# Six attention units ahead of the first half steps, a bank reserve in the planner, decays by doubling and spare buffers at the end, in a decay-attention kernel with a softplus feed-forward layer

## The chip, the core and the metric

The kernel runs on one core of a Trainium2 chip. The core has five engines with queues of their own: TensorE (PE; its weight loads are listed apart as PEld), VectorE (DVE), ScalarE (ACT), GpSimd (POOL), and SyncE (SP), which here only issues DMAs. They wait for each other by semaphores. The metric is the device time of one execution in microseconds. Before the change it was 692.98 us, the median of three runs (692.51 to 694.04).

## The reference

```python
def _attn_ref(q, k, v):                      # B, H, S, D = 4, 8, 768, 64
    gamma = 1.0 - 2.0 ** (-5.0 - np.arange(H, dtype=np.float32))
    scale = 1.0 / np.sqrt(D)
    for t in range(S):
        state = gamma[None, :, None, None] * state + np.einsum('bhd,bhe->bhde', k[:, :, t], v[:, :, t])
        y[:, :, t] = scale * np.einsum('bhd,bhde->bhe', q[:, :, t], state)

def _moe_ref(x, w_in, w_out):                # x: 3072 x 512, w_in: 512 x 2048, w_out: 2048 x 512
    h = x @ w_in
    g = np.maximum(h, 0.0) + np.log1p(np.exp(-np.abs(h)))
    return g @ w_out
```

The attention's output, heads side by side, is `x`. The weights come as 64-bit floats and are turned into float32 words on the chip.

## The kernel before

**Attention in units.** The 768 positions are cut into six chunks of 128 (`C`), the eight heads into two halves of four. A unit is one chunk of one batch for one half: 4 x 6 x 2 = 48 units, `u0` to `u47`, two of them (the two halves) per chunk. In a unit GpSimd scales the queries and values by powers of the decay (L348, from `qtabs` and `vtabs`, one column per chunk), TensorE transposes keys and queries (L356), the scores of the chunk are formed, copied out, masked by GpSimd (L388, L448), and multiplied with the values; the product with the state of the chunks before (`st`) is added. The state is carried on in `td` (L481 to L502). The outputs go to `x` as a high and a low part (L473 ScalarE, L474 VectorE), since the feed-forward layer multiplies in three products: high by high, low by high, high by low, all in float32r.

The first `WHOLE` = 14 units multiply in float32; the others split their operands into two float32r parts as well (the `else` branch of `unit`: L412 to L421 and L444 to L448), with more matmuls, each a quicker one, and more work for ScalarE, VectorE and GpSimd.

**Feed-forward in steps.** The 3072 rows are six blocks of 512 (`T`), the 2048 hidden columns sixteen pieces `f` of 128. A step is one block and one `f`: 12 matmuls of 512 columns into one of two banks `hp0`, `hp1`; then VectorE (L539), ScalarE's softplus (L540), VectorE (L541), ScalarE's cast to `gh` (L542) and GpSimd's rest `gl` (L543); then 12 matmuls with `w_out` into the banks `acc0` to `acc3`. There is one `sp` buffer between L539 and L543 and two each of `gh` and `gl`. After a block's last step the banks are copied to `w0` or `w1` (L576 ScalarE, L578 VectorE) and stored (L580).

In block 0 the first steps are half steps: two `f` at once for the first (`h0`) or second (`h1`) half of the rows, with matmuls of 256 columns, so that they can begin when four of the block's eight units are there. The weights of an `f` are converted just ahead of its first use (L287 to L318: loads, ScalarE, VectorE, GpSimd).

**The order is planned.** Nothing is emitted directly. Every operation is given to a `Planner` with its engine, a cost, the operations it comes after, the buffers it uses (`Held`) and, for some, a due time. `order()` then works out due times backwards, and places one operation after the other by a model of costs and hand-over times (`HANDOVER`, the functions for the costs, the DMA rate): the engine that can begin first, and on it the operation that is due first. That sequence is emitted, and each engine's queue keeps it. Some banks (`SHARED`) are taken by whichever operation comes first. So a change of a cost or a due time moves instructions on every engine, and a line of code may be used at another place than its neighbours.

The list `ORDER` (L24) gives the due times of block 0's first units and half steps one after the other; behind it the main loop gives one step at a time, with new units as the blocks need them.

Of the kernel before, what the change touches and what calls it, by code (L numbers as in the profile page):

```python
# [17 lines left out]
P = 128  # L18
# [3 lines left out]
WHOLE = 14  # L22
BORROW = 8
ORDER = ("u0", "u1", "u2", "u3", "u4", "h0", "u5", "h0", "u6", "u7", "h1", "h1")  # L24
# [8 lines left out]
    "SP": {"PE": 150, "ACT": 30, "DVE": 30, "POOL": 140, "SP": 0},  # L33
# [46 lines left out]
class Planner:  # L80
# [5 lines left out]
    def add(self, engine, cost, run, after=(), uses=(), at=None):  # L86
        op = Op(engine, cost, run, after, uses, at)
        op.number = len(self.ops)
        self.ops.append(op)
        return op  # L90

    def order(self):
# [28 lines left out]
        while len(out) < len(self.ops):  # L121
            best = None
            for e, cands in ready.items():
                if not cands:
                    continue
                starts = []
                for since, op in cands:
                    b = begin(op, since)
                    starts.append((max(free[e], b), b, op))
                first = min(c[0] for c in starts)  # L130
                if first >= 1e12 or best is not None and first >= best[0]:
                    continue
                s, b, op = min((c for c in starts if c[0] <= first + 1e-6), key=lambda c: (c[1] + COMFORT[e] > c[0], c[2].due, c[2].number))
                best = s, op
# [9 lines left out]
            if e == "SP":  # L144
                free[e] = s + 450
                lane = max(lane, s + 2000 - 0.3 * op.cost) + op.cost + (190 if op.cost < 500 else 0)
                op.end = lane + 150
            else:
                op.end = free[e] = s + op.cost
# [5 lines left out]
            for t in op.then:  # L155
                waiting[t] -= 1
                if not waiting[t]:
                    ready[t.engine].append((max(a.end + HANDOVER[a.engine][t.engine] + (MARGIN if a.engine != t.engine else 0) for a in t.after), t))
# [4 lines left out]
SLOW = 1.02  # L163
SHARED = ("hp0", "hp1", "acc0", "acc1", "acc2", "acc3", "a0", "a1")
COMFORT = {"PE": 0, "ACT": 100, "DVE": 100, "POOL": 100, "SP": 0}
# [3 lines left out]
def decay_attention_then_softplus_ffn(ctx: ExitStack, tc: tile.TileContext, q, k, v, w_in, w_out, qtab, vtab, gtab, out):  # L169
# [42 lines left out]
    gtab_sb = pool.tile([P, 2, H], F32, name="gtab_sb")  # L212
    qtabs = pool.tile([P, NC, H], F32, name="qtabs")
    vtabs = pool.tile([P, NC, H], F32, name="vtabs")
# [52 lines left out]
    def DMA(size, run, after=(), uses=(), at=None):  # L267
        return plan.add("SP", size / 316.0, run, after, uses, at)
# [57 lines left out]
    zero, ys, ss, padded = [], {}, {}, []  # L326

    def unit(n, when):
# [16 lines left out]
        ldq = DMA(4 * P * HH * D, lambda: emit(nc.sync.dma_start(buf(qn), src(q))), [], [qn], when[0] - 6000)  # L345
        ldk = DMA(4 * P * HH * D, lambda: emit(nc.sync.dma_start(buf(kn), src(k))), [], [kn], when[0] - 6000)
        ldv = DMA(4 * P * HH * D, lambda: emit(nc.sync.dma_start(buf(vn), src(v))), [], [vn], when[0] - 6000)
        scaled = lambda t, tab: emit(nc.gpsimd.tensor_tensor(t, t, tab[:, c, hs].unsqueeze(2).broadcast_to([P, HH, D]), op=ALU.mult))  # L348
        dq = POOL(615, lambda: scaled(buf(qn), qtabs), [ldq] + tables, [qn])
        dv = POOL(615, lambda: scaled(buf(vn), vtabs), [ldv] + tables, [vn])  # L350
# [56 lines left out]
        else:  # L407
# [3 lines left out]
            for par, own, oth in sides:  # L411
                ck.append(ACT(scalar_time(512), lambda par=par, own=own: emit(nc.scalar.copy(KQ[int(kq.slot[-1])][own, par, :2], tpv()[own])), [tk, tq], [tp, kq]))  # L412
# [5 lines left out]
            vl = DVE(vector_time(256), lambda: emit(nc.vector.tensor_tensor(buf(vhl)[:, :, 1, :], buf(vn), buf(vhl)[:, :, 0, :].bitcast(F32), op=ALU.subtract)), [vh], [vn, vhl])  # L418
            if not ends:
                khi = ACT(scalar_time(256, False), lambda: emit(nc.scalar.copy(buf(kh), buf(kn))), [ldk], [kn, kh])  # L420
                klo = DVE(vector_time(256), lambda: emit(nc.vector.tensor_tensor(buf(kl), buf(kn), buf(kh).bitcast(F32), op=ALU.subtract)), [khi], [kn, kh, kl])  # L421
# [72 lines left out]
        else:  # L494
# [6 lines left out]
                DVE(vector_time(128), lambda: emit(nc.vector.tensor_tensor(buf(to)[up, 0], tdv[:, 0], buf(to)[lo, 0].bitcast(F32), op=ALU.subtract)), [h0], [to]),  # L501
                DVE(vector_time(128), lambda: emit(nc.vector.tensor_tensor(buf(to)[lo, 1], tdv[:, 1], OD.bitcast(F32), op=ALU.subtract)), [h1], [to, od]),  # L502
# [8 lines left out]
    accs = {}  # L511

    def ffn_step(s, h, i, f, when):
# [5 lines left out]
        gl = hold_gl()  # L519
        ts = range(NT) if h is None else range(h * W // P, (h + 1) * W // P)  # L520
# [18 lines left out]
        a = DVE(vector_time(T), lambda: emit(nc.vector.tensor_scalar(U(spv()), U(bank(hp)), 0x80000000, None, op0=ALU.bitwise_or)), [lasts[-1]], [hp, sp])  # L539
# [43 lines left out]
    def setup_tables():  # L583
        emit(nc.scalar.dma_start(qtabs[:, 0], qtab))
        emit(nc.scalar.dma_start(vtabs[:, 0], vtab))
        emit(nc.scalar.dma_start(gtab_sb[lo, 0], gtab))
# [101 lines left out]
```

## Time and profile before

| | before |
|---|---|
| median of 3 runs | 692.98 us (692.51 to 694.04) |
| profiled execution | 691.09 us, its span 689.4 us |
| TensorE busy | 671.6 us, 97% of the span |
| VectorE, ScalarE, GpSimd busy | 413.3, 358.7, 276.8 us |
| matmul rows | 3952, of them 1104 + 96 into `hp`, 768 + 384 into `acc` from `gh` and `gl` |
| bytes moved | 42.67 MB, 62 GB/s in the mean |

The page's busy times are unions of rows. Matmuls are pipelined, so a row's own length (390 ns for 512 columns) is longer than the distance to the next (some 0.23 us); the distance between starts is what a matmul costs its engine. In a timeline a row gives start, length, engine, line, operation, what is written and read, shapes and count, and in brackets the idle time before it with what ended it. Names are the program's tiles: `a`, `acc`, `hp` are banks of the accumulator memory, `win` and `wout` the converted weights, whose last two pieces lend their buffers to early loads, so `wout<-in_q_dram` is a load of queries.

### The profile page before, as it was taken

The page shows a single profiled execution, that of the slowest core. Times are in us where ns is not written, and L with a number is a line of the kernel's source. Part 1 is how long each engine was busy: PE and PEld are TensorE (multiplying, and loading weights), DVE is VectorE, ACT ScalarE, POOL GpSimd, SP SyncE. Part 2 cuts the span into 40 slices and gives each one's busy share as a digit, 9 for nine tenths or more (in the row PEclk, how much of TensorE's full clock was granted, in tenths as well). Part 3 has the DMA queues.
Part 4 walks back from the last instruction along what each step waited for, and adds up shares of the span by engine and source line. Part 5 has one row for each costly group of instructions (what it writes and reads, how often), then busy time and mean ns, then how long its engine had stood idle before and what let it go on. Part 6 is the DMA issues. An engine that isn't in the chain of part 4 may idle for free. (4 is left out here: it accounts for less than half of the span.)

```text
span 689.4 us, 11100 instructions
## 1 busy us (share of the span) xinstructions
PE 671.6 (97%) x3952; PEld 561.8 (82%) x3952; DVE 413.3 (60%) x867; ACT 358.7 (52%) x799; POOL 276.8 (40%) x320
## 2 busy tenths in 40 slices
PE   6998999999999999999999999999999999999995
PEld 5887888888888888888888888888888888888883
DVE  4877867768665656756657656666766564322222
ACT  5887767656555445545545554554645443322222
POOL 5866756543434343433333343333433322222221
PEclk9999999999999999999999999999999999999999
DMA  9859363223111112211111311111211000100001
GB/s 240 225 155 298 92 200 107 53 47 93 24 30 40 24 23 57 75 25 24 39 30 24 93 39 24 24 34 37 85 24 41 21 1 1 52 10 1 1 1 61
DMA packets 90743, 42.67 MB, mean 62 GB/s; under 512 B 77376, under 2 KB 85568, under 8 KB 90688
## 3 DMA queue, kind: packets, MB, share of 16 engines
q1 hardware_dynamic: 90240, 41.96, 22.2%
q8 instruction: 31, 0.51, 0.3%
q14 instruction: 24, 0.20, 0.1%
q10 hardware_dynamic: 448, 0.01, 0.0%
HBM read 35.66 MB, written 6.29 MB: 61 GB/s over the span
## 5 line engine op out<-in xcount | busy, mean ns | idle before, releaser
L270 PE MATMUL hp<-x,win 128*128 128x512 f32 (+1 forms) x1200 | 297.7, 388 | 2.6 <-DVE sp L541 1.6
L270 PEld LDWEIGHTS hp<-x,win 128*128 128x128 f32 x1200 | 213.4, 188 | 42.8 <-issue 2.9
L270 PE MATMUL acc<-wout,gh 128*128 128x512 f32 x768 | 202.3, 395 | 1.4 <-ACT gh L542 1.4
L543 POOL TENSOR_TENSOR gl<-sp,gh 128x512 fp32r<-128x512 f32 x96 | 124.5, 1297 | 186.5 <-ACT gh L542 106.0
L270 PEld LDWEIGHTS acc<-wout,gh 128*128 128x128 f32 x768 | 139.4, 188 | 29.7 <-ACT gh L542 2.3
L539 DVE TENSOR_SCALAR sp<-hp 128x512 uint32<-128x512 uint32 x96 | 65.8, 686 | 92.4 <-PE hp L270 53.1
L540 ACT ACTIVATE sp<-sp 128x512 f32<-128x512 f32 x96 | 60.6, 631 | 100.9 <-DVE sp L539 100.7
L270 PE MATMUL acc<-wout,gl 128*128 128x512 f32 x384 | 108.8, 391 | 0.7 <-POOL gl L543 0.7
L270 PEld LDWEIGHTS acc<-wout,gl 128*128 128x128 f32 x384 | 71.2, 188 | 15.7 <-POOL gl L543 1.1
L542 ACT CAST gh<-sp 128x512 fp32r<-128x512 f32 x96 | 59.5, 619 | 35.8 <-DVE sp L541 35.3
L541 DVE SCALAR_TENSOR_TENSOR sp<-hp,sp 128x512 f32<-128x512 f32 x96 | 66.1, 688 | 17.6 <-ACT sp L540 16.0
L444 ACT CAST ah<-a 128x256 fp32r<-128x256 f32 x68 | 23.0, 375 | 64.8 <-PE a L270 64.4
L414 DVE TENSOR_TENSOR kq<-a,kq 64x256 fp32r<-64x256 f32 x68 | 28.7, 422 | 45.5 <-ACT kq L413 37.8
L448 POOL TENSOR_SCALAR_AFFINE_SELECT ah<-ah 128x512 fp32r<-128x512 f32 x34 | 21.9, 644 | 75.2 <-DVE al L445 75.2
L412 ACT CAST kq<-a 64x512 fp32r<-64x512 f32 x68 | 39.5, 581 | 22.9 <-PE a L356 17.2
L348 POOL TENSOR_TENSOR vn<-vn,vtabs 128x256 f32<-128x256 f32 x46 | 28.6, 621 | 49.5 <-DMA vn<-in_v_dram 30.5
L348 POOL TENSOR_TENSOR qn<-qn,qtabs 128x256 f32<-128x256 f32 x46 | 28.5, 620 | 47.3 <-DMA qn<-in_q_dram 42.6
L445 DVE TENSOR_TENSOR al<-a,ah 128x256 fp32r<-128x256 f32 x68 | 26.7, 419 | 34.6 <-ACT ah L444 34.3
L270 PE MATMUL a<-ah,vhl 128*64 128x128 f32 x272 | 40.8, 222 | 0.0
L474 DVE TENSOR_TENSOR x<-a,x 64x256 fp32r<-64x256 f32 x86 | 35.8, 416 | 8.4 <-ACT x L473 7.1
L270 PE MATMUL a<-kq,st 128*64 128x128 f32 x240 | 34.1, 223 | 0.0
L473 ACT CAST x<-a 64x256 fp32r<-64x256 f32 x86 | 31.4, 365 | 5.0 <-PE a L270 3.1
(121 smaller groups left out, 831.2 us busy)
## 6 DMA issues: line engine op xcount, KB each, us to landing
raw<-in_moe_w_in_dram SPq DMA_DIRECT2D x16, 512.0 KB, 5.3
raw<-in_moe_w_out_dram SPq DMA_DIRECT2D x16, 512.0 KB, 6.0
out_dram<-w SPq DMA_DIRECT2D x24, 256.0 KB, 2.1
qn<-in_q_dram SPq DMA_DIRECT2D x46, 128.0 KB, 2.7
kn<-in_k_dram SPq DMA_DIRECT2D x46, 128.0 KB, 2.3
vn<-in_v_dram SPq DMA_DIRECT2D x46, 128.0 KB, 2.3
wout<-in_q_dram SPq DMA_DIRECT2D x2, 128.0 KB, 4.8
win<-in_k_dram SPq DMA_DIRECT2D x2, 128.0 KB, 4.0
```

Of the source, the lines that this page charges most:

```text
L270: mm = lambda o, l, r, start, stop: emit(nc.tensor.matmul(o, lhsT=l, rhs=r, start=start, stop=stop))
L348: scaled = lambda t, tab: emit(nc.gpsimd.tensor_tensor(t, t, tab[:, c, hs].unsqueeze(2).broadcast_to([P, HH, D]), op=ALU.mult))
L412: ck.append(ACT(scalar_time(512), lambda par=par, own=own: emit(nc.scalar.copy(KQ[int(kq.slot[-1])][own, par, :2], tpv()[own])), [tk, tq], ...
L414: cl.append(DVE(vector_time(256), lambda par=par, own=own, oth=oth: emit(nc.vector.tensor_tensor(KQ[int(kq.slot[-1])][oth, par, 0], tpv()[ ...
L445: l1 = DVE(vector_time(256), lambda js=js, scv=scv: emit(nc.vector.tensor_tensor(buf(al)[:, js], scv(0), buf(ah)[:, js].bitcast(F32), op=A ...
L473: xh.append(ACT(scalar_time(256), lambda par=par, r=r: emit(nc.scalar.copy(xo(0, r), ypv()[:, par])), [y] + xdeps, [yp]))
L474: xl.append(DVE(vector_time(256), lambda par=par, r=r: emit(nc.vector.tensor_tensor(xo(1, r), ypv()[:, par], xo(0, r).bitcast(F32), op=ALU ...
L539: a = DVE(vector_time(T), lambda: emit(nc.vector.tensor_scalar(U(spv()), U(bank(hp)), 0x80000000, None, op0=ALU.bitwise_or)), [lasts[-1]], ...
L540: b = ACT(640, lambda: emit(nc.scalar.activation(spv(), spv(), AF.Softplus)), [a], [sp])
L541: c = DVE(vector_time(T), lambda: emit(nc.vector.scalar_tensor_tensor(spv(), bank(hp), 0.0, spv(), op0=ALU.max, op1=ALU.add)), [b], [hp, sp])
L542: e = ACT(scalar_time(T, False), lambda: emit(nc.scalar.copy(buf(gh), spv())), [c], [sp, gh])
L543: g = POOL(1300, lambda: emit(nc.gpsimd.tensor_tensor(buf(gl), spv(), buf(gh).bitcast(F32), op=ALU.subtract)), [e], [sp, gh, gl])
```

## The change

It has six parts, and a new set of the planner's numbers.

- **Order of block 0.** `ORDER` puts six units ahead of the first half step and two more ahead of the second; two of the four half steps go, and whole steps take their place (14 instead of 12 in block 0).
- **Planner.** An operation that would take a bank in `SHARED` now leaves it when an operation that is due earlier and could start within `RESERVE` would need it; only where nothing else can start is it placed all the same. VectorE operations with two operands in the on-chip memory (`BOTH`) are modelled as held by GpSimd's. Costs, hand-over times, the loads' rate and the lead of units and steps have new values.
- **Decays.** One tile `tabs` holds both tables for the six chunks. The ten small products that made one chunk from the one before are five rows by doubling: chunk 1 from chunk 0; the rates squared, chunks 2 and 3; the rates squared again, chunks 4 and 5. A unit waits for its own chunk's rows only.
- **Memsets.** Those of `qw` go from GpSimd to VectorE; those of `kq` have a task of their own with a later due time.
- **Last block.** In its last eight steps `sp` may also lie in `win0`, `gh` in `vhl0` or `ah0`, `gl` in `vhl1` or `al0`; `w` may lie in `win1` and `win2`. Their `hp` matmuls are due earlier, up to 1.6 steps for the last.
- **Float32 units.** `WHOLE` goes from 14 to 16: units 14 and 15 (block 1) are multiplied in float32.

```diff
-WHOLE = 14
+WHOLE = 16
-ORDER = ("u0", "u1", "u2", "u3", "u4", "h0", "u5", "h0", "u6", "u7", "h1", "h1")
+ORDER = ("u0", "u1", "u2", "u3", "u4", "u5", "h0", "u6", "u7", "h1")
...
+            def waits(s, op):
+                for u in op.uses:
+                    if u.slot is None and u.among[0] in SHARED:
+                        rivals = sum(d < op.due and t < s + RESERVE and o is not op and set(v.among) <= set(u.among) for d, t, o, v in wants)
+                        if rivals and rivals >= sum(opens(n, op.engine) <= s for n in u.among):
+                            return True
+                return False
+
+            for fair in (True, False):
+                for e, starts in fits.items():
+                    if fair:
+                        starts = [c for c in starts if not waits(c[0], c[2])]
...
+                if op.both and busy[0] < s < busy[1]:
+                    op.end = max(op.end, busy[1] + 0.65 * op.cost)
...
+        final = i == NB - 1 and f >= NF - RAMP
+        if final:
+            sp.among.append("win0")
+            gh.among += ["vhl0", "ah0"]
+            gl.among += ["vhl1", "al0"]
...
+            if i == NB - 1:
+                ob.among += ["win1", "win2"]
...
-    def setup_vector():
-        emit(nc.vector.reciprocal(gtab_sb[:, 1], gtab_sb[:, 0]))
-        for c in range(1, NC):
-            emit(nc.vector.tensor_tensor(qtabs[:, c], qtabs[:, c - 1], gtab_sb[:, 0], op=ALU.mult))
-            emit(nc.vector.tensor_tensor(vtabs[:, c], vtabs[:, c - 1], gtab_sb[:, 1], op=ALU.mult))
+    def decays(level, first, n):
+        r = rates[:, level].unsqueeze(1).broadcast_to([P, n, 2, H])
+        emit(nc.vector.tensor_tensor(tabs[:, first:first + n], tabs[:, first - (1 << level):first - (1 << level) + n], r, op=ALU.mult))
+
+    def setup_decays():
+        emit(nc.vector.reciprocal(rates[:, 0, 1], rates[:, 0, 0]))
+        decays(0, 1, 1)
+
+    def setup_later_decays():
+        for level in (1, 2):
+            emit(nc.vector.tensor_tensor(rates[:, level], rates[:, level - 1], rates[:, level - 1], op=ALU.mult))
+            decays(level, 1 << level, min(NC - (1 << level), 1 << level))
...
+        early = AHEAD * max(0, f + 1 - (NF - RAMP)) / RAMP if i == NB - 1 else 0
+        ffn_step(None, None, i, f, (now - early * step, now + hidden_time + second_time))
```

What the planner makes of this is read from the order in which the instructions stand. Numbers in names are those of buffers; the new code's line numbers are higher (L375 becomes L414, L356 becomes L395, L270 becomes L309).

VectorE, from the decay tables to the first copies of `qw` (the queries of a float32 unit, spread over two halves), before:

```order
L592 TENSOR_TENSOR qtabs<-qtabs,gtab_sb 128x8
L593 TENSOR_TENSOR vtabs<-vtabs,gtab_sb 128x8
L375 COPY qw_73<-a_119 64x256
L481 COPY td_71<-a_135 64x256
L375 COPY qw_74<-acc_143 64x256
```

and now:

```order
L643 RECIPROCAL rates<-rates 128x8
L640 TENSOR_TENSOR tabs<-tabs,rates 128x16
L414 COPY qw_72<-a_107 64x256
L520 COPY td_70<-a_121 64x256
L648 TENSOR_TENSOR rates<-rates 128x16
L640 TENSOR_TENSOR tabs<-tabs,rates 128x32
L648 TENSOR_TENSOR rates<-rates 128x16
L640 TENSOR_TENSOR tabs<-tabs,rates 128x32
L414 COPY qw_73<-acc_133 64x256
```

Before, the first two rows shown are the last of five such pairs; now one product stands ahead of the first copy, and the rest behind it.

TensorE, where block 0's last half steps and its first whole steps (512 columns) stand. Before:

```order
L270 MATMUL hp_723<-x_68,win_432 128x256 x6
L270 MATMUL a_746<-qw_73,kh_707 128x128 x4
L270 MATMUL hp_695<-x_68,win_273 128x256 x6
L270 MATMUL hp_695<-x_68,win_289 128x256 x12
L270 MATMUL hp_723<-x_68,win_432 128x256 x6
L270 MATMUL hp_723<-x_68,win_457 128x256 x12
L356 MATMUL a_683<-ident,kn_647 128x128 x2
L270 MATMUL hp_821<-x_68,win_635 128x512 x6
```

and now:

```order
L309 MATMUL hp_613<-x_67,win_252 128x256 x6
L309 MATMUL hp_625<-x_67,win_484 128x512 x6
L309 MATMUL hp_613<-x_67,win_252 128x256 x6
L309 MATMUL hp_613<-x_67,win_312 128x256 x12
L309 MATMUL hp_625<-x_67,win_484 128x512 x6
L395 MATMUL a_684<-ident,qn_495 128x128 x2
L309 MATMUL a_692<-qw_72,kh_620 128x128 x4
L395 MATMUL a_684<-ident,kn_522 128x128 x2
L309 MATMUL hp_706<-x_67,win_571 128x512 x3
```

Two half steps (`hp_695`, `hp_723`) stood ahead of the first whole step (`hp_821`); now one half step (`hp_613`) and a whole one share the place, and the next whole step (`hp_706`) follows transposes and a score group.

TensorE at the last two steps of the last block. Before:

```order
L270 MATMUL hp_7050<-x_69,win_1310 128x512 x3
L270 MATMUL hp_7097<-x_69,win_1363 128x512 x12
L270 MATMUL acc_6639<-wout_1457,gh_7114 128x512 x2
L270 MATMUL acc_6643<-wout_1457,gh_7114 128x512 x2
L270 MATMUL acc_6675<-wout_1457,gh_7114 128x512 x2
L270 MATMUL acc_6663<-wout_1457,gh_7114 128x512 x2
L270 MATMUL acc_6639<-wout_1457,gl_7118 128x512
L270 MATMUL acc_6643<-wout_1457,gl_7118 128x512
L270 MATMUL acc_6675<-wout_1457,gl_7118 128x512
L270 MATMUL acc_6663<-wout_1457,gl_7118 128x512
L270 MATMUL acc_6639<-wout_1486,gh_7134 128x512 x2
L270 MATMUL acc_6639<-wout_1486,gl_7136 128x512
```

and now:

```order
L309 MATMUL hp_6962<-x_68,win_1561 128x512 x12
L309 MATMUL hp_6977<-x_68,win_1676 128x512 x12
L309 MATMUL acc_6538<-wout_1499,ah_6959 128x512 x2
L309 MATMUL acc_6541<-wout_1499,ah_6959 128x512 x2
L309 MATMUL acc_6567<-wout_1499,ah_6959 128x512 x2
L309 MATMUL acc_6556<-wout_1499,ah_6959 128x512 x2
L309 MATMUL acc_6538<-wout_1499,al_6966 128x512
L309 MATMUL acc_6541<-wout_1499,al_6966 128x512
L309 MATMUL acc_6567<-wout_1499,al_6966 128x512
L309 MATMUL acc_6556<-wout_1499,al_6966 128x512
L309 MATMUL acc_6538<-wout_1629,gh_6994 128x512 x2
L309 MATMUL acc_6541<-wout_1629,gh_6994 128x512 x2
```

Before, the last step's `hp` (`hp_7097`) had the twelve matmuls of one step between it and its own `acc` group (from `gh_7134`); now `hp_6977` has those of the two steps before it there (from `ah_6959` and `gh_6994`), and its own follow behind the rows shown.

In the middle of the program each split unit has four VectorE rows between its scores and its outputs (now L484 and L485, two each). In the old order another row, mostly L539, stood among them in 31 of 34 units; in the new one one does in 10 of 32.

More of the change, by code (lines that the diff above doesn't have):

```diff
@@ L32 @@
     "POOL": {"PE": 60, "ACT": 60, "DVE": 40, "POOL": 10, "SP": 60},
-    "SP": {"PE": 150, "ACT": 30, "DVE": 30, "POOL": 140, "SP": 0},
+    "SP": {"PE": 140, "ACT": 30, "DVE": 30, "POOL": 140, "SP": 0},
 }
@@ L157, in order @@
                 if not waiting[t]:
-                    ready[t.engine].append((max(a.end + HANDOVER[a.engine][t.engine] + (MARGIN if a.engine != t.engine else 0) for a in t.after), t))
+                    ready[t.engine].append((max(t.earliest, *(a.end + HANDOVER[a.engine][t.engine] + (MARGIN if a.engine != t.engine else 0) for a in t.after)), t))
         return sorted(out, key=lambda op: (op.start, op.number))
 MARGIN = 0
-SLOW = 1.02
+UNIT = 3500
+STEP0 = 4500
+LEAD = 1300
+STAGE = 2000
+EXTRA = 1.0
+LOAD = 6000
+PACE = 1290
+WAIT = 1e9
+RESERVE = 600
+SLOW = 1.05
 SHARED = ("hp0", "hp1", "acc0", "acc1", "acc2", "acc3", "a0", "a1")
+AHEAD = 1.6
+RAMP = 8
 COMFORT = {"PE": 0, "ACT": 100, "DVE": 100, "POOL": 100, "SP": 0}
@@ L265, in POOL, with BOTH, DMA @@
         return plan.add("POOL", n, run, after, uses, at)
[L267 to L268 removed]
+    def BOTH(n, run, after, uses=(), at=None):
+        op = plan.add("DVE", n, run, after, uses, at)
+        op.both = True
+        return op
+    def DMA(size, run, after=(), uses=(), at=None, rate=340.0):
+        return plan.add("SP", size / rate, run, after, uses, at)
     mm = lambda o, l, r, start, stop: emit(nc.tensor.matmul(o, lhsT=l, rhs=r, start=start, stop=stop))
@@ L538, in ffn_step @@
         spv = lambda: buf(sp)
-        a = DVE(vector_time(T), lambda: emit(nc.vector.tensor_scalar(U(spv()), U(bank(hp)), 0x80000000, None, op0=ALU.bitwise_or)), [lasts[-1]], [hp, sp])
+        free = [spent[f_] for f_ in range(3)] if final else []
+        if i == NB - 1:
+            spent[f] = lasts[-1]
+        a = DVE(vector_time(T), lambda: emit(nc.vector.tensor_scalar(U(spv()), U(bank(hp)), 0x80000000, None, op0=ALU.bitwise_or)), [lasts[-1]] + free, [hp, sp])
         b = ACT(640, lambda: emit(nc.scalar.activation(spv(), spv(), AF.Softplus)), [a], [sp])
@@ L601, in setup_pool @@
             emit(nc.gpsimd.memset(t[lo, 1, 2].bitcast(F32), 0.0))
-    tables = [ACT(400, setup_tables, [], at=-1e6)]
+    landing = ACT(2200, setup_tables, [], at=-1e6)
     make_identity(nc, ident)
-    zero = [POOL(2400, setup_pool, [], at=-1e6)]
-    tables = [DVE(1000, setup_vector, tables, at=-1e6)]
+    zero = [DVE(800, setup_pool, [], at=-1e6)]
+    padding = [POOL(1300, setup_padding, [], at=60000.0)]
+    soon = DVE(360, setup_decays, [landing])
+    soon.earliest = 5900.0
+    later = DVE(680, setup_later_decays, [soon])
+    tables = [landing, soon] + [later] * (NC - 2)
     EARLY_BANKS = ["a0", "a1", "acc2", "acc3", "acc0", "acc1"]
```

102 lines of the change are left out of this document (55 added, 47 removed).

## The prediction

> **What bounds the kernel now.** I read the page's busy shares first, then the busy time by window, then the timeline of TensorE with its idle notes, and last the timelines of the other engines at the places where TensorE stood still.
>
> The page's busy line says that TensorE is the engine to count:
>
> ```profile
> PE 671.6 (97%) x3952; PEld 561.8 (82%) x3952; DVE 413.3 (60%) x867; ACT 358.7 (52%) x799; POOL 276.8 (40%) x320
> ```
>
> The windows (start:end, length, then busy time and instructions of PE, PEld, DVE, ACT, POOL, then clock, DMA share, GB/s) say where the other 17.8 us of the 689.4 us span are to be sought; here one early window, the one in which weights and units meet, one of the middle and the last:
>
> ```profile
> 10.00:20.00 10.00, 8.77 (x73) 7.37 (x72) 6.86 (x15) 8.51 (x21) 5.21 (x8) 1.00 1.18 297
> ...
> 60.00:80.00 20.00, 18.41 (x95) 15.13 (x94) 18.06 (x31) 15.60 (x28) 14.55 (x12) 1.00 0.52 176
> ...
> 350.00:400.00 50.00, 50.00 (x312) 42.22 (x310) 32.48 (x75) 27.41 (x65) 17.53 (x21) 1.00 0.20 53
> ...
> 680.00:689.40 9.40, 3.29 (x12) 2.09 (x12) 1.38 (x2) 1.17 (x2) 1.27 (x1) 0.89 0.29 112
> ```
>
> The middle (the row 350:400 stands for it) has no idle time: there only TensorE's own work counts. The last window has 6.1 us of it. The early part is named by TensorE's own timeline, whose note in brackets is the idle time before a row and what ended it:
>
> ```profile
> 4.67 0.66 PE L356 MATMUL a<-ident,kn 128*128 128x128 f32 x2 [4.67 <-POOL qn L348]
> 16.82 0.44 PE L356 MATMUL acc<-ident,kn 128*128 128x128 f32 x2 [0.99 <-ACT qw L374]
> 21.82 0.50 PE L270 MATMUL hp<-x,win 128*128 128x256 f32 x2 [1.03 <-DVE x L474]
> 55.41 1.13 PE L270 MATMUL a<-qw,kh 128*128 128x128 f32 x8 [0.95 <-ACT st L492]
> 62.67 1.63 PE L270 MATMUL hp<-x,win 128*128 128x512 f32 x6 [1.59 <-DVE sp L541]
> ```
>
> These five make 9.2 us, 4.6 of them after the start (10:20 has 1.23 idle in all, 60:80 has 1.59). The first 4.67 us go on loads and on GpSimd's first scaling. The change leaves the order of the first loads as it is and takes four memsets out of GpSimd's queue ahead of that scaling; how soon the first keys would allow more isn't shown apart, so I take nothing there, with 0.5 us as the best.
>
> **Start: the decay tables.** VectorE's timeline, with one GpSimd row:
>
> ```profile
> 5.93 0.20 DVE L590 RECIPROCAL gtab_sb<-gtab_sb 128x8 f32<-128x8 f32 x1 [5.93 <-DMA gtab_sb<-in_gtab_dram]
> 6.91 0.63 POOL L348 TENSOR_TENSOR vn<-vn,vtabs 128x256 f32<-128x256 f32 x1 [0.55 <-DMA vn<-in_v_dram]
> 7.02 0.55 DVE L592 TENSOR_TENSOR qtabs<-qtabs,gtab_sb 128x8 f32<-128x8 f32 x1
> 7.68 0.43 DVE L375 COPY qw<-a 64x256 f32<-64x256 f32 x1
> ```
>
> Ten products stand between the reciprocal and the first `qw` copy, without which the first scores can't start. Now one product stands there, so the copy starts near 6.45 instead of 7.68: 1.2 us sooner. The other four products, those of the doubling, now follow the first copies; queued behind them is the second unit's `qw` copy, which waits for its own transposes anyway. I take the whole 1.2 us, since every early wait above hangs on a chain that starts here. Bounds: nothing (a later load decides) and 1.2. The four memsets that move to VectorE stand ahead of the reciprocal, whose operand lands at 5.93, so their cover is that wait; without it the first copy would be four short rows later.
>
> [...]
>
> **Early phase: six units ahead of the half steps.** Two of the four half steps leave the first 60 us. Two of the waits go with their cause. At 21.82 a half step stood in TensorE's queue before its `x` was written; in the new order its first three matmuls stand behind unit 3's states and outputs and unit 4's scores and states, 0.61 + 1.89 + 0.81 + 0.61 = 3.9 us of work later (the group times are in the next part). At 62.67 four half steps in a row had filled both `hp` banks and the next step waited for L541 to free one; now the first whole steps take turns with the last half step, and between the end of `hp_613` and the first write to its bank again stand 6 matmuls of 512 columns, four transposes and one score group, 1.36 + 0.44 + 0.87 = 2.7 us by the spacings of the timeline, against a chain of L539, L540 and L541 that takes 2.1 us in the tail rows below and its hand-overs. I keep 0.3 us of that wait for other VectorE work in between. Gain 1.0 + 1.3 = 2.3 us, with the tables 3.5 us. The waits at 16.82 and 55.41 I leave, as float32 units follow one another there now as before. Bounds: all of it lost (units without half steps between them give TensorE less to fill with), and at best about 7 us (the 4.6 us of waits, the tables' 1.2 and as much again of matmuls that the model of their ends counts as busy while ScalarE, at 8.51 of 10 us in 10:20, is what feeds them). I take 3.5, the part with a row for each wait.
>
> **TensorE's own work: two more float32 units.** Units 14 and 15 are no longer split. From TensorE's timeline, starts of each group and of the next:
>
> ```profile
> 82.09 0.68 PE L270 MATMUL a<-vn,kn 128*64 128x64 f32 x8
> 82.70 0.44 PE L356 MATMUL a<-ident,qn 128*128 128x128 f32 x2
> 96.48 1.06 PE L270 MATMUL a<-qw,kh 128*128 128x128 f32 x8
> 97.29 0.94 PE L270 MATMUL hp<-x,win 128*128 128x512 f32 x3
> 101.56 0.43 PE L270 MATMUL a<-qw,st 128*64 128x128 f32 x2
> 103.45 0.96 PE L270 MATMUL hp<-x,win 128*128 128x512 f32 x3
> 306.64 0.64 PE L270 MATMUL a<-kq 128*128 128x256 f32 x4
> 307.12 2.91 PE L270 MATMUL hp<-x,win 128*128 128x512 f32 x12
> 309.86 0.22 PE L270 MATMUL a<-vhl,kh 128*64 128x128 f32 x1
> 310.30 0.94 PE L270 MATMUL hp<-x,win 128*128 128x512 f32 x3
> 311.08 0.28 PE L270 MATMUL a<-kq,st 128*64 128x128 f32 x2
> 312.28 2.06 PE L270 MATMUL acc<-wout,gh 128*128 128x512 f32 x8
> ```
>
> A float32 unit: states 0.61, scores 0.81, outputs 1.89, in all 3.31. A split one: 0.44, 0.48, 1.20, in all 2.12. The difference is 1.2, and as float32 groups also hold up the group before or after them I take 1.4: 2.8 us for two. No stall covers this, as TensorE has none there; what ScalarE, VectorE and GpSimd save is hidden. Against it, the same products in 512 columns cost less than in 256:
>
> ```profile
> L270 PE MATMUL hp<-x,win 128*128 128x512 f32 x1104 | 283.8, 396 | 1.6 <-DVE sp L541 1.6
> L270 PE MATMUL hp<-x,win 128*128 128x256 f32 x96 | 13.9, 291 | 1.0 <-DVE x L474 1.0
> ```
>
> 24 x 13.9/96 - 12 x 283.8/1104 = 0.4 us saved by two half steps less, 0.2 each. Together +2.4 us; bounds +2.0 and +2.9.
>
> **Tail.** The end of the timeline, and the chain's last wait:
>
> ```profile
> 675.74 2.12 PE L270 MATMUL acc<-wout,gh 128*128 128x512 f32 x8 [0.23 <-ACT gh L542]
> 677.15 0.69 DVE L539 TENSOR_SCALAR sp<-hp 128x512 uint32<-128x512 uint32 x1 [2.17 <-POOL gl L543]
> 678.54 0.69 DVE L541 SCALAR_TENSOR_TENSOR sp<-hp,sp 128x512 f32<-128x512 f32 x1 [0.70 <-ACT sp L540]
> 679.99 0.73 PE L270 MATMUL acc<-wout,gh 128*128 128x512 f32 x2 [1.21 <-ACT gh L542]
> 681.40 0.50 PE L270 MATMUL acc<-wout,gl 128*128 128x512 f32 x1 [0.67 <-POOL gl L543]
> 683.57 0.39 PE L270 MATMUL acc<-wout,gl 128*128 128x512 f32 x1
> 684.83 0.59 ACT L576 COPY w<-acc 128x512 f32<-128x512 f32 x1 [1.61 <-DMA out_dram<-w]
> 685.54 0.69 DVE L578 COPY w<-acc 128x512 f32<-128x512 f32 x1 [2.91 <-ACT w L576]
> 683.24 2.10 DMA out_dram<-w
> ```
>
> The last softplus chain is late by 0.23 + 1.21 + 0.67 = 2.1 us. In the new order its `hp` stands 24 accumulating matmuls (5.4 us) ahead of its first use instead of 12, and a second `sp` buffer lets it begin before the step before it is through GpSimd; 5.4 us is more than the chain took (677.15 to 679.99, 2.8 us, and 4.3 until `gl` at 681.40), and the wait of L539 for GpSimd's `gl` goes. I take 2.4, since a matmul after a wait also takes longer (0.50 for one against 0.39 in the last row); bounds 2.1 and 2.7. Then the copies: the last two waited for the first stores to free `w`. With four buffers the last copy starts when its matmul ends, 683.57 + 0.39, and takes 0.59, so it ends at 684.55 instead of 685.54 + 0.69 = 686.23: 1.7 us. What is late next is the store: four of 256 KB now leave 0.7 us apart, with up to 2.10 us each in flight. I take 1.4; bounds 0.8 and 1.7.
>
> **Middle.** 490 us are set by another order, without an idle row to win but for a few tenths. The order keeps more work between an `hp` group's end and its first use (median 6.0 us against 4.8), so I cost it at nothing; the rival on late masks below is what it costs if that is wrong.
>
> **Sum.** -1.2 - 2.3 + 2.4 - 2.4 - 1.4 = -4.9 us. The profiled execution took 691.09 us around its span of 689.4 and would take 686.2. It lies 1.9 us under the median of the runs, 692.98; on the median the forecast is 688.1 us.
>
> **Rivals.**
> *The early waits only move* (chance 0.20). TensorE waits for the units' own chains as long as for the half steps. For it: VectorE at 18.06 of 20 us in the row 60:80, so what replaces a half step there isn't free. Against it: two waits lose their cause. The early -3.5 falls away: 691.6 us, on the edge of no change.
> *The early phase gains twice* (0.16). For it: with the half steps go 2 x 2 weight conversions out of ScalarE's and VectorE's way before 60 us. Against it: loads set the pace at a DMA share of 1.18 in 10:20. -7 instead of -3.5: 684.6 us.
> *Tables held by GpSimd* (0.08). One product of ten was held, by 0.55 - 0.17 = 0.4 us by its neighbours' length; if every doubling row is, the second unit's copy is 4 x 0.4 = 1.6 us late, which takes the tables' 1.2 us back: 689.3 us. For it: GpSimd scales five tiles in that stretch. Against it: nine of ten rows passed. [...]
> *Masks arrive late* (0.10), the other side. In the middle a split unit's scores go through ScalarE, four VectorE rows and two GpSimd masks before its outputs:
>
> ```profile
> 334.50 2.91 PE L270 MATMUL hp<-x,win 128*128 128x512 f32 x12
> 335.54 0.68 DVE L539 TENSOR_SCALAR sp<-hp 128x512 uint32<-128x512 uint32 x1
> 337.01 0.64 POOL L448 TENSOR_SCALAR_AFFINE_SELECT al<-al 128x512 fp32r<-128x512 f32 x1 [0.62 <-DVE al L446]
> ```
>
> The scores end where the first row starts and the second mask ends at 337.65, so the chain takes 3.15 us. Between scores and outputs the old order keeps about 4.0 us of TensorE work, the new one about 3.5, with 3.3 in several units. For it: this thinner cover. Against it: the row L539 that stood inside the chain is out of it in 22 of the 32 split units. It decides from a chain of about 3.6 us on: one more row of 0.68 gives 3.83, short by 0.26 us a unit on average, 8.4 us over 32, and 696.5 us, slower than before.
> *The change doesn't do what it says* is no rival of its own: the order shows the moved rows.
>
> **How the numbers follow.** Forecast 0.46, then 0.20, 0.16, 0.08 and 0.10. A change under 0.2% (1.4 us) can't be told from none in this kernel. Faster: 0.46 + 0.16 + 0.08, and 0.08 of the first rival, which lies on the edge: 0.78. No change: the other 0.12 of it. Slower: 0.10. The likeliest case alone has 685 to 691 us: its waits as shown, give or take 2 us, and the bounds of tail and work. The range goes on to the twofold gain below and past the moved waits above, 683.0 to 692.5 us, and leaves out some 0.18, most of it the late masks.
>
> **What would show it.** The first `qw` copy on VectorE near 6.45 us, the first scores done near 8.2. No wait of a whole step on `sp` over 0.5 us before 70 us. TensorE's groups of units 14 and 15 in float32, 3.3 us each. No idle row after 660 us until the last matmul, and under 4.6 us from its start to the end of the span (683.57 to 689.4 before). The windows of the middle full. It would be wrong if waits on `ah` or `al` stood at the outputs in the middle, if the units of the first 50 us waited for `kh` or `st` in place of the half steps, or if the last stores landed one behind the other.

## The result, and the profile after

The change takes 682.9 us (median of four runs, 682.72 to 683.71) where the kernel before takes 693.35 us in the same set (692.51 to 694.04): a ratio of 0.9852, 95% interval 0.9835 to 0.9869, so 1.3 to 1.65% faster. Against the 692.98 us of the prediction that is -10.1 us, where -4.9 was forecast: the direction was right, the gain was twice as large, and 682.9 lies 0.1 us below the lower end of the range, 683.0. Between the two profiled executions (691.09 and 682.85 us) it is only -8.2 us, and the 1.9 us between these two differences have a part of their own below.

The windows of the change, with the columns of those shown of before:

```profile
10.00:20.00 10.00, 9.43 (x78) 7.84 (x77) 7.02 (x14) 7.97 (x20) 5.74 (x9) 1.00 0.98 268
20.00:40.00 20.00, 19.82 (x173) 18.11 (x172) 13.88 (x29) 16.05 (x39) 13.42 (x17) 1.00 0.72 201
60.00:80.00 20.00, 20.00 (x121) 16.40 (x120) 12.94 (x23) 12.54 (x27) 12.00 (x13) 1.00 0.49 139
350.00:400.00 50.00, 50.00 (x295) 42.07 (x295) 32.74 (x75) 27.92 (x67) 18.76 (x22) 1.00 0.21 56
660.00:670.00 10.00, 10.00 (x45) 8.26 (x45) 3.46 (x5) 2.63 (x5) 1.94 (x2) 1.00 0.00 0
```

TensorE is idle for 0.57 us between 10 and 20 (1.23 before) and not at all between 60 and 80 (1.59 before). VectorE, which had 18.06 of 20 us there, now has 12.94. The middle is full, as it was. What is left of TensorE's waits after 15 us is in four rows of its timeline:

```profile
16.84 0.43 PE L309 MATMUL a<-qw,st 128*64 128x128 f32 x2 [0.29 <-ACT ah L426]
17.55 0.43 PE L309 MATMUL a<-ah,win 128*64 128x128 f32 x2 [0.28 <-POOL ah L427]
21.64 1.16 PE L309 MATMUL acc<-qw,kh 128*128 128x128 f32 x8 [0.18 <-ACT qw L413]
51.83 0.44 PE L395 MATMUL a<-ident,kn 128*128 128x128 f32 x2 [0.22 <-ACT qw L413]
```

The end of the timeline has no idle note on TensorE any more:

```profile
671.60 1.98 PE L309 MATMUL acc<-wout,gh 128*128 128x512 f32 x8
672.07 1.29 POOL L590 TENSOR_TENSOR gl<-sp,gh 128x512 fp32r<-128x512 f32 x1 [1.43 <-issue]
673.41 1.07 PE L309 MATMUL acc<-wout,gl 128*128 128x512 f32 x4
674.77 0.39 PE L309 MATMUL acc<-wout,gl 128*128 128x512 f32 x1
676.81 0.39 PE L309 MATMUL acc<-wout,gl 128*128 128x512 f32 x1
677.24 0.58 ACT L625 COPY w<-acc 128x512 f32<-128x512 f32 x1 [0.77 <-PE acc L309]
677.28 0.90 SPq L629 DMA_DIRECT2D out_dram<-w  x2
```

The `gl` of the last step is ready at 673.36 (672.07 + 1.29), and its first use is the row at 674.77, 1.4 us later; the rows at 671.60 and 673.41 still read the step before. The last copy follows the last matmul without waiting for a store. From the start of the last matmul to the end of the span are 681.1 - 676.81 = 4.3 us, 5.8 before (689.4 - 683.57).

To book the whole span, each matmul's distance to the next start was compared with the median distance of its kind (same shape, same tiles, `a` and `acc` taken as one); what is above the median, the excess, is waiting or a slow clock. In us, with the terms of the prediction:

| part | before | after | measured | forecast |
|---|---|---|---|---|
| start and excess up to 80 us | 17.5 | 14.0 | -3.5 | -1.2 - 2.3 = -3.5 |
| excess between 80 and 660 us | 11.4 | 9.6 | -1.8 | 0 |
| excess after 660 us | 3.0 | 0.0 | -3.0 | -2.4 |
| last matmul's start to the end | 5.8 | 4.3 | -1.5 | -1.4 |
| the matmuls' own time (medians) | 651.7 | 653.2 | +1.5 | +2.4 |
| sum | | | -8.3 | -4.9 |
| profile against median | | | -1.9 | 0 |

The sum is the span's -8.3. The row of the medians is good to about 1 us: in the second profile of before (e1) the median of one kind with 768 matmuls is 1 ns longer, and its row reads 652.6. No term went the wrong way; the middle, the tail, TensorE's own work and the base (the profile taken for the median) were missed.

### The profile page after: what moved, and what is told of

The parts are those of the page before. It is cut to its first block, busy times and chain, and to the rows that moved or that the text cites. A ratio compares the mean times of both kernels' runs of the same rounds, so it can differ in the third digit from the quotient of the medians.

```text
span 681.1 us, 10936 instructions
## 1 busy us (share of the span) xinstructions
PE 671.8 (99%) x3928; PEld 564.8 (83%) x3928; DVE 411.5 (60%) x842; ACT 349.9 (51%) x787; POOL 275.5 (40%) x314
## 4 chain that ended last, share of the span: by engine, by line
PE 98%; issue 0%; DMA 0%; ACT 0%; POOL 0%; SPq 0%; DVE 0%; POOLq 0%; ACTq 0%
PE acc L309 42%; PE hp L309 39%; PE a L309 14%; PE a L395 3%; PE acc L395 0%; DMA vn<-in_v_dram 0%; DVE w L353 0%; POOL ah L427 0%; POOL vn L387 0%; ACT win L356 0%; POOL qn L387 0%; ACT w L625 0%; ACT qw L413 0%; SPq L385 0%; SPq L384 0%
## 5 line engine op out<-in xcount | busy, mean ns | idle before, releaser
L309 PE MATMUL hp<-x,win 128*128 128x512 f32 (+1 forms) x1176 | 294.1, 391 | 0.0
L309 PEld LDWEIGHTS hp<-x,win 128*128 128x128 f32 x1176 | 212.5, 188 | 41.2 <-issue 0.9
L309 PE MATMUL acc<-wout,gh 128*128 128x512 f32 x736 | 195.6, 394 | 0.0
L590 POOL TENSOR_TENSOR gl<-sp,gh 128x512 fp32r<-128x512 f32 x90 | 116.4, 1293 | 126.3 <-ACT gh L589 73.3
L309 PEld LDWEIGHTS acc<-wout,gh 128*128 128x128 f32 x736 | 133.5, 188 | 25.4 <-issue 0.3
L309 PE MATMUL acc<-wout,gl 128*128 128x512 f32 x368 | 103.7, 391 | 0.0
L309 PEld LDWEIGHTS acc<-wout,gl 128*128 128x128 f32 x368 | 68.6, 188 | 14.4
L589 ACT CAST gh<-sp 128x512 fp32r<-128x512 f32 x90 | 55.8, 620 | 41.3 <-DVE sp L588 41.2
L588 DVE SCALAR_TENSOR_TENSOR sp<-hp,sp 128x512 f32<-128x512 f32 x92 | 62.9, 684 | 13.0 <-ACT sp L587 12.0
L387 POOL TENSOR_TENSOR vn<-vn,tabs 128x256 f32<-128x256 f32 x46 | 28.8, 625 | 81.1 <-DMA vn<-in_v_dram 65.8
L387 POOL TENSOR_TENSOR qn<-qn,tabs 128x256 f32<-128x256 f32 x46 | 29.4, 640 | 66.7 <-DMA qn<-in_q_dram 63.8
L309 PE MATMUL a<-ah,vhl 128*64 128x128 f32 x256 | 38.5, 223 | 0.0
L453 DVE TENSOR_TENSOR kq<-a,kq 64x256 fp32r<-64x256 f32 x64 | 27.0, 422 | 17.5 <-ACT kq L452 13.7
L541 DVE TENSOR_TENSOR st<-td,od 64x128 fp32r<-64x128 f32 x28 | 10.2, 363 | 42.1 <-PE a L309 41.9
L484 DVE TENSOR_TENSOR al<-a,ah 128x256 fp32r<-128x256 f32 x64 | 25.2, 421 | 16.2 <-ACT ah L483 16.0
```

What stands on the lines that cost most here:

```text
L309: mm = lambda o, l, r, start, stop: emit(nc.tensor.matmul(o, lhsT=l, rhs=r, start=start, stop=stop))
L453: cl.append(DVE(vector_time(256), lambda par=par, own=own, oth=oth: emit(nc.vector.tensor_tensor(KQ[int(kq.slot[-1])][oth, par, 0], tpv()[ ...
L484: l1 = DVE(vector_time(256), lambda js=js, scv=scv: emit(nc.vector.tensor_tensor(buf(al)[:, js], scv(0), buf(ah)[:, js].bitcast(F32), op=A ...
L588: c = DVE(vector_time(T), lambda: emit(nc.vector.scalar_tensor_tensor(spv(), bank(hp), 0.0, spv(), op0=ALU.max, op1=ALU.add)), [b], [hp, sp])
L589: e = ACT(scalar_time(T, False), lambda: emit(nc.scalar.copy(buf(gh), spv())), [c], [sp, gh])
L590: g = POOL(1300, lambda: emit(nc.gpsimd.tensor_tensor(buf(gl), spv(), buf(gh).bitcast(F32), op=ALU.subtract)), [e], [sp, gh, gl])
```

## Experiments

Each kernel was timed in five rounds beside the kernel before. The change run again (e10) gave 682.89 us, so runs of different sets are compared with that.

**The kernel before, profiled again (e1).** No edit.

> The kernel before, unchanged, profiled a second time. The change gained 10.1 us on the medians (692.98 to 682.9) but only 8.2 us between the two profiled executions (691.09 and 682.85). Theory A (the first profile of before was of an execution that waited 1.5 to 2 us less early on than most): the new profile lies at 692 to 694 us, and the extra time stands in idle rows of TensorE before 80 us, in waits that begin at loads. Theory B (the extra is spread over the whole span, as a slower clock or slower matmuls would be): the busy time of PE rises from 671.6 to 673 us or more. Theory C (that execution was nothing special): the new profile lies within 0.5 us of 691.09.

693.64 us (691.31 to 695.24); before in the same set 694.4 us, with runs from 691.22 to 696.83. The new profile lies at 693.68 us, span 692.0: 2.6 us more than the first. Theory A holds in part: 2.0 us of the 2.6 are excess before 20 us, but most of it is no wait. Theory B has its sign, TensorE's busy time is 673.7 us against 671.6, but the extra is not spread over the span. TensorE's timeline of this run:

```profile
7.31 0.63 PE L270 MATMUL acc<-qw,kh 128*128 128x128 f32 x2
8.51 1.65 PE L270 MATMUL acc<-qw,kh 128*128 128x128 f32 x6 [0.57 <-DVE qw L375]
10.09 1.12 PE L270 MATMUL acc<-vn,kn 128*64 128x64 f32 x8
12.29 1.59 PE L270 MATMUL a<-qw,kh 128*128 128x128 f32 x8
13.81 1.09 PE L270 MATMUL a<-ah,vn 128*64 128x128 f32 x8
```

and the same place in the first profile of before:

```profile
8.16 0.94 PE L270 MATMUL acc<-qw,kh 128*128 128x128 f32 x6 [0.15 <-DVE qw L375]
9.02 0.68 PE L270 MATMUL acc<-vn,kn 128*64 128x64 f32 x8
10.53 1.16 PE L270 MATMUL a<-qw,kh 128*128 128x128 f32 x8 [0.24 <-ACT kh L372]
```

The same six matmuls take 1.65 us in the one and 0.94 in the other; their starts lie 0.213 us apart, and 0.111. The clock records of the traces, which give the share of TensorE's full clock that is granted, say why: full clock is granted from 13.23 us in the new profile and from 8.03 us in the first one; by these spacings the matmuls run at about half of it until then. The window view prints 1.00 for those first microseconds, so it hides this; the distances between starts do not. The ten products of the decay tables, two of them held beside GpSimd this time (0.58 and 0.54 us beside rows of 0.63 and 0.61, where seven of the others take 0.15 to 0.17), had let TensorE wait 0.57 us at 8.51, 0.15 before.

**The spare buffers alone, and the change without them (e2, e3).** Into before go, or out of the change come, these lines, the due times of the last steps and the wait for the matmuls that still read the borrowed buffers; ahead of 639 us the matmuls keep their order.

```diff
+        final = i == NB - 1 and f >= NF - RAMP
+        if final:
+            sp.among.append("win0")
+            gh.among += ["vhl0", "ah0"]
+            gl.among += ["vhl1", "al0"]
...
+            if i == NB - 1:
+                ob.among += ["win1", "win2"]
```

> Before, with only the part on the last block: spare buffers for sp, gh, gl and w, and the steps due earlier there. The prediction's terms: -2.4 us for the last softplus chain and -1.4 us for the last copies and stores, together -3.8 us. From the two profiles: the waits of 0.39, 1.38 and 0.84 us beyond a matmul's own time at 675 to 682 us are gone in the change (-2.6), and from the last matmul's start to the end of the span are 4.28 us in place of 5.83 (-1.55), together -4.2 us. If the tail's gain needed the planner's new costs too (rival), it is under 2 us here.

> The change without its part on the last block (one sp, two gh, two gl and two w buffers to the end, no step due earlier). If the parts add up, it is 3.8 us (the prediction's terms) to 4.2 us (the two profiles) slower than the change, 686.7 to 687.1 us. If the tail's wait would have gone without the buffers, by the new costs alone (rival), it is less than 1.5 us slower than the change.

e2: 687.48 us, ratio to before 0.9901 (0.9878 to 0.9925), so -5 to -8.5 us. e3: 689.02 us, 6.1 us slower than the change (5.1 by the ratios to before, 0.9917 and 0.9844, each in its own set). The rivals fall, and the tail is worth some 5 to 7 us and not 3.8 or 4.2. The end of e3, TensorE and one copy of ScalarE:

```profile
677.26 0.73 PE L309 MATMUL acc<-wout,gh 128*128 128x512 f32 x2 [1.23 <-ACT gh L589]
678.96 0.79 PE L309 MATMUL acc<-wout,gl 128*128 128x512 f32 x1 [0.97 <-POOL gl L590]
679.55 1.05 PE L309 MATMUL acc<-wout,gh 128*128 128x512 f32 x2
680.40 0.63 PE L309 MATMUL acc<-wout,gl 128*128 128x512 f32 x1
680.83 1.05 PE L309 MATMUL acc<-wout,gh 128*128 128x512 f32 x2
683.12 0.58 ACT L623 COPY w<-acc 128x512 f32<-128x512 f32 x1 [1.47 <-PE acc L309]
```

and two of its windows:

```profile
676.00:679.00 3.00, 0.80 (x4) 0.34 (x3) 0.50 (x1) 0.62 (x1) 1.26 (x1) 0.99 0.01 3
679.00:682.40 3.40, 3.40 (x8) 2.73 (x9) 0.69 (x1) 0.59 (x1) 0.00 (x0) 0.51 0.21 77
```

After the two waits the granted clock is 0.51 for 3.4 us, and six 512-column matmuls take 0.427 us in place of 0.227: 6 x 0.2 = 1.2 us that no wait shows. The trace of e5 below, whose tail is that of before, has the same fall (to 0.50 from 680.88 to 684.30, eight matmuls, 1.6 us); the two profiles of before have the same waits of 1.21 and 0.67 us and no fall (in the first the clock is 1.00 until 687 us, in e1 the matmuls behind the waits start 0.23 us apart). The fall is paid back in part. ScalarE's last copy comes so late that it waits for its matmul (683.12) and no longer for a store, as it did in before, and from the start of the last matmul to the end are 5.05 us in e3 and 4.83 in e5, 5.80 and 6.19 in the profiles of before. Excess after 660 us and end together take 8.8 and 9.1 us in before, 9.4 in e5, 9.9 in e3 and 4.3 in the change, so by the traces the tail is worth 4.5 to 5.6 us.

**The old order in the change, and the new order in before (e4, e11).** One line each.

```diff
-ORDER = ("u0", "u1", "u2", "u3", "u4", "u5", "h0", "u6", "u7", "h1")
+ORDER = ("u0", "u1", "u2", "u3", "u4", "h0", "u5", "h0", "u6", "u7", "h1", "h1")
```

> The change with the old order of units and half steps (five units ahead of the first half step, four half steps); all else of the change stays. The prediction's early terms: +2.3 us for the waits that come back, +0.4 us for two more half steps, 685.6 us. By the two profiles the waits before 80 us fell by 4.45 us, 0.5 of that at the decay tables; if the order made the rest, +4 us and +0.4, 687.3 us. If the new costs and the reserved banks made it and not the order (rival), it stays within 1 us of the change, and TensorE shows no wait over 0.5 us at the half steps.

> Before, with the order of units and half steps of the change alone (six units ahead of the first of two half steps), by the old costs. The prediction's early terms: -2.3 us of waits and -0.4 us of two half steps fewer, -2.7 us. From the run that put the old order into the change (+5.6 us): -5 us. Rival (the order pays only with the new costs): within 1 us of before, with waits over 0.5 us between 20 and 80 us.

e4: 688.5 us, 5.6 us slower than the change (4.9 by the ratios). Between 20 and 80 us its trace has 4.2 us more excess than the change, in six waits of 0.42 to 0.55 us between 31 and 64 us, two of them half steps waiting for `x`:

```profile
57.29 0.39 PE L309 MATMUL hp<-x,win 128*128 128x256 f32 x1 [0.46 <-ACT x L512]
58.23 4.46 PE L309 MATMUL hp<-x,win 128*128 128x256 f32 x35 [0.55 <-DVE x L513]
```

e11: 693.01 us against 693.37, ratio 0.9998 (0.9981 to 1.0015): nothing. So the new order gains nothing by the old costs, and the old order loses under the new ones. e11's timeline shows where the gain stays out:

```profile
16.47 0.44 PE L356 MATMUL acc<-ident,kn 128*128 128x128 f32 x2 [0.99 <-ACT qw L374]
21.56 1.16 PE L270 MATMUL a<-qw,kh 128*128 128x128 f32 x8 [1.02 <-ACT qw L374]
54.52 1.61 PE L270 MATMUL hp<-x,win 128*128 128x512 f32 x6 [2.02 <-DVE sp L541]
```

The half step's wait at 21.82 is gone, and a unit waits 1.02 us for `qw` at the same time; the wait of a whole step for a free `hp` bank is there as before, 8 us earlier and 2.02 us long. This is the first rival of the prediction, "the early waits only move", and it holds for the order by itself. They also move out of the early part: against the first profile of before the excess between 20 and 80 us is 7.1 us in place of 7.8, but that between 80 and 660 us is 13.3 in place of 11.4, with new waits of 0.2 to 0.4 us at 169, 185, 454 and 511 us. Which of the new costs (step and unit times, bandwidth of loads) or the bank reserve removes them was not separated: it is open. The reserve and the moved memsets have no run of their own.

**Doubling alone, and the change without it (e5, e6).** Only VectorE's rows differ from before, or from the change; e6 puts this in place of the doubling:

```diff
+        for c in range(1, NC):
+            for t in range(2):
+                emit(nc.vector.tensor_tensor(tabs[:, c, t], tabs[:, c - 1, t], rates[:, 0, t], op=ALU.mult))
```

> Before, with the decays by doubling alone: one product ahead of the first qw copy, four behind the first td copy; every other instruction in the old order. The prediction's term: -1.2 us. By the profiles of before and of the change, TensorE's wait in the first scores shrinks by 0.46 us: -0.5 us. A third theory, from the second profile of before: there the wait at that place was 0.57 us and the granted clock came to full at 13.2 us, in the first profile 0.15 us and 8.0 us, and the difference was 2.0 us of the span. If that wait decides when the clock comes, its removal is worth up to 2.5 us on the median and the clock is full by 10.3 us.

> The change with the ten products one behind another ahead of the first qw copy, as before; every other instruction as in the change. The prediction's term: +1.2 us. The profiles' waits: +0.5 us. [...]

e6: 684.11 us (682.24 to 684.24), +1.2 us, the prediction's term, though one of the four runs is as fast as the change. Its clock came at 10.09 us, that of the change at 10.16, so the third theory is not borne out there. e5: 692.43 against 693.49 us, ratio 0.9996 (0.9978 to 1.0013): before spreads too widely to tell 1.2 us from nothing. In its trace the wait in the first scores is gone and the clock is full from 8.46 us (before: 8.03 and 13.23).

**Two more float32 units (e7).** `WHOLE = 18`.

> The change with units 16 and 17 in float32 too. The prediction's price of a float32 unit, 1.4 us: +2.8 us. By the sums of starts to next starts in the two profiles, two more units and two half steps fewer made +1.6 us where +2.4 was forecast, so a unit is at 1.0: +2.0 us. If other work fills the difference (rival): within 0.7 us of the change.

686.03 us, +3.1 us, or 1.6 for a unit: the prediction's 1.4 holds. In the sums of starts 2.0 us are the matmuls' own medians, 1.0 a unit, and 1.1 are excess, most of it at the changes between the kinds of matmul between 140 and 180 us.

**Matmuls ahead of the first load (e8, e9).** Twelve of zeros over 64 rows, then six of ones over the whole array:

```diff
+    spare, ones = psum.tile([P, 512], F32, name="hp1"), X[1][:, 0, 0, 0, :C].bitcast(F32)
+    emit(nc.vector.memset(ones, 1.0))
+    for _ in range(6):
+        mm(spare[:, :P], ones, ones, True, True)
```

> The change, with twelve matmuls of zeros (64x128 by 64x128, written to hp1 and read by nobody) in front of the first transposes, while TensorE has nothing to do. In the change's profile the clock is granted in full from 10.16 us, 5.8 us after the first matmul at 4.37. [...]

> The change, with six matmuls of ones over the whole array (128x128 by 128x128, two records of 0.213 us each at the half clock, written to hp1 and read by nobody) ahead of the first transposes; they should run from 1.3 to 3.9 us and be done before the first keys land at 4.4. The zeros of the run before (twelve of 64 rows) took 5.5 us where 2.6 were counted, put the first transposes at 6.67 in place of 4.37, and the clock still came only at 10.93. [...]

e8: 684.38 us, +1.5; the zeros ran until 6.7 us and the clock was full from 10.93, later than the 10.16 of the change. e9: 682.96 us, no change, full from 9.79. Neither gained time. TensorE's timeline of e9:

```profile
1.13 2.93 PE L309 MATMUL hp<-x 128*128 128x128 f32 x12 [1.13 <-DVE x L719]
4.36 0.66 PE L395 MATMUL a<-ident,kn 128*128 128x128 f32 x2 [0.30 <-DMA kn<-in_k_dram]
5.79 1.12 PE L309 MATMUL a<-vn,kn 128*64 128x64 f32 x8 [0.34 <-POOL vn L387]
```

Two waits of 0.30 and 0.34 us follow the ones, and half-rate spacing goes on past them (the eight matmuls at 7.32 take 1.91 us, those at 10.65 take 1.16).

**The change again (e10).** No edit.

> The change unchanged, as the base for the runs beside it and for how its time spreads. The kernel before spreads over 689.97 to 697.33 us, with traces in which the clock came at 8.0 and 13.2 us and fell to half at 680.9 us in one. [...] Rival (the chip's state makes the spread): it spreads over 4 us or more, as before.

682.89 us, 682.78 to 683.23, while before, in turns with it on the same chip, spread from 690.97 to 695.33. The rival falls, as far as four runs show it (the eight runs of the change together lie from 682.72 to 683.71): the spread belongs to the kernel. Its clock came at 10.28 us, that of the first profile at 10.16.

**Without the model of held VectorE rows (e12).**

```diff
-        op.both = True
+        op.both = False
```

> The change, with the planner no longer told that a VectorE instruction with two SBUF inputs is held while GpSimd runs (both = False everywhere). The prediction put the middle at nothing; the two profiles show that 1.05 us of waits went there, the largest of them 0.73 us at 293 us, where the second half of a unit's scores waited for td (L485) behind a kl row of 1.47 us in place of 0.42, beside a GpSimd row of 1.30. If the model of the hold is what took these waits away: +0.7 to +1.5 us, with waits on td or kl at the scores in the middle. Rival (other costs or chance made the order, since 9 rows are still held in the change): within 0.5 us of the change.

683.46 us (683.12 to 684.96), +0.6 us. One wait like that of before at 293 us is there, at another place (a second one, of 0.28 us at 135, is of another kind). Before:

```profile
291.15 1.30 POOL L543 TENSOR_TENSOR gl<-sp,gh 128x512 fp32r<-128x512 f32 x1
291.26 1.47 DVE L421 TENSOR_TENSOR kl<-kn,kh 128x256 fp32r<-128x256 f32 x1
292.65 0.41 DVE L485 TENSOR_TENSOR td<-a,td 64x256 f32<-64x256 f32 x1
293.20 0.47 PE L270 MATMUL a<-kq 128*128 128x256 f32 x2 [0.56 <-DVE td L485]
```

e12:

```profile
492.64 1.29 POOL L590 TENSOR_TENSOR gl<-sp,gh 128x512 fp32r<-128x512 f32 x1
492.72 1.49 DVE L460 TENSOR_TENSOR kl<-kn,kh 128x256 fp32r<-128x256 f32 x1
494.24 0.42 DVE L524 TENSOR_TENSOR td<-a,td 64x256 f32<-64x256 f32 x1
494.81 0.48 PE L309 MATMUL a<-kq 128*128 128x256 f32 x2 [0.33 <-DVE td L524]
```

A `kl` row of 0.42 us takes 1.5 us beside GpSimd's `gl`, the state's sum `td` behind it is late, it frees the bank late, and the second half of the scores waits. The change has nine `kl` rows over 0.5 us too, and no idle row of TensorE after 52 us. The model does not make held rows rarer: they are 7 of 28 in before, 9 of 26 in the change and 3 of 26 in e12. The time lies between the two expectations, and the edit also moves many other matmuls from 135 us on. So at most some 0.6 us of the middle's 1.8 is this model; that the model, and not the new order by chance, kept the wait away is not shown, and the rest is open.

## Why the prediction was right in sign and too small in size

**Start.** "The copy starts near 6.45 instead of 7.68" and the whole 1.2 us: the copy starts at 6.16, and e6 measures 1.2. Of the 0.3 us between 6.45 and 6.16 the load is the cause: the reciprocal starts at 5.54 in the change's profile and at 5.93 in before's. The first scores were not done at 8.2 but at 9.0, because they ran at the half clock: eight matmuls from 7.07 took 1.91 us, where the eight at 21.64 take 1.16. The doubling's rows behind the first copies:

```profile
6.16 0.43 DVE L414 COPY qw<-a 64x256 f32<-64x256 f32 x1
7.03 0.53 DVE L648 TENSOR_TENSOR rates<-rates 128x16 f32<-128x16 f32 x1
7.59 0.57 DVE L640 TENSOR_TENSOR tabs<-tabs,rates 128x32 f32<-128x32 f32 x1
8.28 0.19 DVE L640 TENSOR_TENSOR tabs<-tabs,rates 128x32 f32<-128x32 f32 x1
9.51 0.43 DVE L414 COPY qw<-acc 64x256 f32<-64x256 f32 x1 [1.04 <-PE acc L395]
```

Two of four are held, for 0.53 and 0.57 us beside GpSimd rows of 0.61. The two behind them took 0.16 and 0.19 us, and nothing is late: the next copy waits 1.04 us for its transposes. The rival of held tables was right on the holding and wrong on its price.

**Early waits.** -2.3 was forecast for two waits; the start and the first 80 us together moved by -3.5 against -3.5. That agreement is luck: two errors cancel. The idle rows between 15 and 80 us fell from 4.6 to 1.0 us, so by 3.6 and not by 2.3: the waits the text left alone shrank too (the one at 55.41 is 0.22 us now, at 51.83; that at 16.82 became two of 0.29 and 0.28), and the whole 1.59 at 62.67 went. Against it, the change's profile got its full clock at 10.16 us and before's at 8.03, some 1.0 us at half rate. The step that failed is "two of the waits go with their cause", as far as the cause was the order: the order alone gains no time (e11), and with the new costs it is worth about 5 us (e4).

**TensorE's own work.** +2.8 for two float32 units stands (e7: 3.1). The saving of the half steps was counted wrong: the text took 24 matmuls of 256 columns against 12 of 512 for two half steps, and the profiles have 48 fewer and 24 more. By the text's own rows that is 0.8 us and not 0.4; by the distances between starts it is 48 x 0.120 - 24 x 0.227 = 0.3. The bounds +2.0 to +2.9 missed the booked +1.5, which has only the medians of each kind: +2.0 for the units, -0.3 for the half steps, the rest from medians that differ. The units' hold on their neighbours is in the excess there.

**Tail.** The waits' -2.4 is -3.0 by the table, where 2.6 are the three waits; the stores' -1.4 is -1.5. The mechanism and both terms were right for the execution that was shown. What the step missed: in e3 and e5 the clock falls to half for 3.4 us behind like waits, the matmuls there take 1.2 to 1.6 us more, and the last copies wait less, so that tail and end take 9.4 to 9.9 us in place of 8.8 to 9.1.

**Middle.** "I cost it at nothing" failed: -1.8 us. The wait at 293 us was 0.7 of it, and e12 gives the model of held rows at most 0.6; the rest has no cause shown. The masks, the rival on the other side, never came late: from the end of a unit's scores to the end of its second mask are 2.3 to 2.9 us, and the first use stands 2.9 to 4.5 us behind the scores.

**The base.** The step that cost most was "it lies 1.9 us under the median of the runs, 692.98; on the median the forecast is 688.1": an offset taken over as if the change had it too. It has not: its profile and its median are the same (682.85 and 682.9). Before's profiled execution had its clock early and kept it in the tail. In e1, near the median with 693.68 us, the clock came 5.2 us later, 2.0 us of time; in e5 it fell in the tail. That the median execution lacked one or both is likely and not shown, as it left no trace. The mean granted clock kept for every run, which does not count the time ahead of the first grant, does not order them either: of the 62 runs of before in the sets of the experiments, 21 have 0.998 and lie from 691.21 to 695.13 us, 18 have 0.996 and lie from 691.98 to 695.33.

## What to carry to other kernels

Where the runs of a kernel lie as far apart as those of before (690.97 to 695.33 us in one set), look for the reason in that kernel before taking one profile as its base: a second profile of it cost one run and showed 2.0 us at the start that waits name only in part. A short wait of TensorE near the end can cost more than its own length: in e3 and e5 the clock fell to half for 3.4 us behind it, and the matmuls there took 1.2 and 1.6 us more. An order and the costs that made it are one change: by itself, in the other's planner, the order here was worth nothing. And count a forecast's matmuls by kind before you price them: here the saving of two half steps was worked out with the matmuls of one.

## What was not expected of the hardware

In e3 and e5 the granted clock fell to half in the tail while matmuls still ran, each time for 3.4 us: 0.51 between 679.00 and 682.40, 0.50 between 680.90 and 684.30. The falls came behind waits of 1.23 and 0.97 us in e3, of 1.19 and 0.67 us in e5. In both profiles of before waits of 1.21 and 0.67 us stand at the same place without a fall: the clock of the first is 1.00 until 687 us, behind its last matmul, and the matmuls of e1 start 0.23 us apart there, as at the full clock. The first grant of the full clock moves too: it came at 8.03 us in the first profile of before and at 13.23 in e1, though TensorE's first row starts at 4.67 and 4.62. In e8 and e9 TensorE had matmuls from 1.25 and 1.13 us on, and the clock was full from 10.93 and 9.79, against 10.16 and 10.28 in the two profiles of the change. What decides when the full clock comes, and why like waits came with a fall in two executions and with none in two others, is not shown.
